# Attention steps of batches 4 to 7 moved half an output stage earlier and reordered, with four more seven-product pairs, in a fused attention and bilinear-FFN kernel

## The chip, the cores and the metric

The kernel runs on one core of a Trainium2 chip. A core has TensorE (matmuls, PE in the profile, weight loads PEld), VectorE (DVE), ScalarE (ACT), GpSimd (POOL) and SyncE (SP), each with its own instruction stream, which it works through in the order in which the program lists it; semaphores make one engine wait for another. The metric is the device time of one execution in microseconds (us), the median of several runs.

## The reference

Sparse attention for 8 batches of 8 heads (576 tokens, head size 64), then a bilinear feed-forward block over all 4608 tokens:

```python
scores = scale * np.matmul(q, k.transpose(0, 1, 3, 2))
rel = pos[:, None] - pos[None, :]
mask_local = (rel >= 0) & (rel < stride)                       # heads 0 to 3
mask_strided = (rel >= 0) & (pos[None, :] % stride == pos[:, None] % stride)   # heads 4 to 7
attn = softmax of the masked scores
x = (attn @ v), heads side by side: 4608 x 512
out = ((x @ w_a) * (x @ w_b)) @ w_out          # 512 -> 1536 -> 512
```

## The kernel before

**Feed-forward.** The tokens are cut into nine tiles of 512 (t = 0 to 8). A tile has sixteen slots, numbered 16t to 16t+15 in one list that the loop at L1122 walks. Slots 0 to 11 are the *ab stage* (`ffn_ab`, L620): slot f makes the 128-wide column block f of x@w_a and x@w_b, eight matmuls of 512 columns, ScalarE copies the first bank out (L638) and VectorE multiplies it with the second into `pf` (L641). Slots 12 to 15 are the *output stage* (`ffn_ys`, L930, with `y_plan`, L871): 84 matmuls of 256 columns (L886) in fourteen blocks of six, in the order of `Y_ORDER` (L859). "y n" below is the point after block n. ScalarE copies and VectorE adds between the blocks; the sums that these products need (`fast_s`) are made by VectorE during the ab stage.

**Seven-product pairs.** For some pairs g of column blocks (2g and 2g+1) the x@w_a half is made from seven half-size products instead of eight (a Strassen-Winograd scheme over two halves of the tokens and two of the 512 inputs): 14 matmuls of 256 columns in place of 8 of 512; the x@w_b half stays as it is. `a_pair_mid` (L676) does it in tiles 3 to 6 where `MID_A` (L28) lists g, with its shared bank `X` in the PSUM pool "e" of one buffer; `a_pair` (L736) does it in tiles 7 and 8 (`FAST_A`). ScalarE makes five copies of 256 columns instead of two of 512, and VectorE three more additions (L710). Products of differences of x need `xsum` (L668), four VectorE subtractions a tile.

**Attention.** The attention of batch b = 3 to 7 is threaded into the feed-forward matmuls of tile b-1. Its steps have letters: `S`u (L425) scores of unit u, that is matmuls into the one bank "st", an exp on ScalarE and a mask on VectorE; `V`u (L490) the product with v. Units 0 to 3 are local heads: V writes PSUM bank "o" and VectorE takes a reciprocal (L470) and multiplies out of the bank into `xl` (L488). Units 4 to 7 are strided heads (`step_VT`, L510): V writes banks "o" and "e", ScalarE does Ln, Ln, Exp (L533, L534), VectorE two products into `xT` (L536). From tile 3 on "o" and "e" have one buffer each. `Q`0 and `Q`1 copy the transposed q of the local heads into the two halves of the zero-padded buffer `qz` that S0 to S3 read, `Q`2 and `Q`3 those of the strided heads, for S4 to S7 (`step_Q`, L334, VectorE, L338). `O`c and `I`c (L500, L506) send the local result through DRAM and back, transposed, into `xT`, on SP's queue. `step_D` (L321), on the same queue, brings kT and qT by transposing DMAs. The loads of k, q and v are issued by GpSimd, which first copies one element of the slot's result (`pace`, L1134) to wait for it.

**What sets the order.** `tc.manual_schedule` keeps the order in which the code emits instructions, on every engine. In one slot come the matmuls and their copies, with the "y n" steps inside an output stage as they are reached (L893); then `soon` (fast_s), then the steps of `LATER` at that slot (`take`, L1137), then the entries of `at` (L1138: fast_s, xsum, stores, step_D). A key x of `LATER` stands for slot 16(b-1)+x, so -4 is slot 12 of tile b-2; `IN_Y` gives points inside the output stage of tile b-1.

Of the kernel before, what the change touches and what calls it, by code (L numbers as in the profile page):

```python
# [14 lines left out]
FIRST_D = 2  # L15
# [9 lines left out]
VW = 128  # L25
WCH = (0, 2, 5, 9, 12)
FAST_Y = (1, 2, 3, 4, 5, 6, 7, 8)
MID_A = {t: (1, 3) for t in (3, 4, 5, 6)}  # L28
FAST_A = {7: (1, 2, 3, 4, 5), 8: (0, 1, 2, 3, 4, 5)}


@with_exitstack
def kernel(
# [20 lines left out]
    NT = n_tok // TTOK  # L54
# [279 lines left out]
    def step_Q(b, z, j):  # L334

        r = slice(64 * j, 64 * j + 64)
        dst = qz_buf[b % 2][j][z][r]
        nc.vector.tensor_copy(dst.rearrange("d c r n -> d (c r n)") if z else dst, qT[z][r])  # L338
# [220 lines left out]
    def step_X(b, c):  # L559
# [15 lines left out]
    STEPS = {1: {5.5: "Tk2", 6: "Tq2", 7: "S4 Tk3", 7.5: "S5", 8: "Tq3", 8.5: "V4", 9: "S6 V5 Pk0", 9.5: "S7 Pq0",  # L575
# [4 lines left out]
    LATER = {-4: "Q0", -3: "Q1", -1: "S0", 0: "S1", 1: "V0", 2: "S2 Q2", 3: "V1 O0", 4: "S3 I0 Q3", 5: "V2", 6: "S4", 7: "V3 O1", 8: "S5", 9: "V4 I1",  # L580
             10: "S6",
             11: "V5"}
    IN_Y = {2: "S7", 6: "V6", 11: "V7"}
    FN = {"Tk": step_Tk, "Tq": step_Tq, "S": step_S, "V": step_V, "X": step_X, "W": lambda b, n: fast_w(n, slice(0, 3)),
          "s": S_px, "m": S_m, "L": lead_vl, "O": rows_out, "I": rows_in, "Pk": lambda b, c: pair_up("k", c), "Pq": lambda b, c: pair_up("q", c),
          "Q": lambda b, n: step_Q(b, n // 2, n % 2)}

    def run(b, slot):
        for s in slot:
# [3 lines left out]
    steps = {}  # L593
# [9 lines left out]
    def mm_bank(shape):  # L603
        nm = "tp" if used[0] % 4 == 3 and used[0] >= 0 else "mm"
        used[0] += 1
        return psum4[nm].tile(shape, F32, tag=nm, name="mm")
# [13 lines left out]
    def ffn_ab(t, f, mid, ab=None):  # L620
        if f == 0:
            pfs[t] = fsb.tile([128, FD, TTOK], BF16, tag="pf", name="pf", bufs=1)
        pf = pfs[t]
        if f // 2 in FAST_A.get(t, ()) + MID_A.get(t, ()):
            if f % 2 == 0:
                pairs[t, f // 2] = (a_pair_mid if t in MID_A else a_pair)(t, f // 2)
            return next(pairs[t, f // 2])
# [14 lines left out]
        else:  # L642
# [5 lines left out]
    xsum = {t: qz_flat[1][t - 7][:, :8 * HT].rearrange("p (n c m) -> p n c m", n=4, c=2)  # L648
            for t in FAST_A}
    xsum_mid = const.tile([128, 4, 2, HT], BF16, name="xsum")  # L650
    for t in MID_A:
        xsum[t] = xsum_mid
# [15 lines left out]
    def xsum_make(t, n):  # L668
        s_ = xsum[t]
        a, b = ((x_part(t, 0, 1), x_part(t, 0, 0)), (x_part(t, 1, 1), s_[:, 0]), (x_part(t, 1, 1), x_part(t, 0, 1)),  # L670
                (x_part(t, 1, 0), s_[:, 1]))[n]
        nc.vector.tensor_tensor(s_[:, n], a, b, op=ALU.subtract)
# [3 lines left out]
    def a_pair_mid(t, g):  # L676

        pf = pfs[t]
        X = psum4["e"].tile([128, 512], F32, tag="e", name="e")[:, :HT]
        Y, Z, b1, b0 = [mm_bank([128, TTOK]) for _ in range(4)]  # L680
        Y, Z = Y[:, :HT], Z[:, :HT]
        a = [fsb.tile([128, TTOK], F32, tag="a_sb", name="a_sb", bufs=3) for _ in range(2)][::-1]
        p7 = fsb.tile([128, HT], F32, tag="p7", name="p7")
        quarter = lambda e, k: a[e][:, HT * k:HT * (k + 1)]

        def P(bank, lhs, rhs, start=False):
            for c in range(2):
                nc.tensor.matmul(bank, lhsT=lhs(c), rhs=rhs(c), start=start and c == 0, stop=c == 1, skip_group_check=True)

        w = lambda e, j: (lambda c: wav[:, j, c, g, e])  # L690
        ws = lambda n: (lambda c: wsum_a[n][:, c, g])
        x = lambda j, k: (lambda c: x_part(t, j, k)[:, c])
        xs = lambda n: (lambda c: xsum[t][:, n, c])

        def b_mm(bank, e, kks):
            f = 2 * g + e
            x0 = TTOK * t % (XR * S)
            for kk in kks:
                for k in range(2) if x0 + TTOK > XR * S else (None,):
                    rhs = x_part(t, kk // 2, k)[:, kk % 2] if k is not None else xT[:, kk, x0:x0 + TTOK]  # L700
                    dst = bank if k is None else bank[:, HT * k:HT * (k + 1)]
                    nc.tensor.matmul(dst, lhsT=wb_sb[:, kk, 128 * f:128 * (f + 1)], rhs=rhs,  # L702
                                     start=kk == 0 and k in (None, 0), stop=kk == KD - 1 and k in (None, 1))

        def mult(e, bank):
            halves = lambda v_: v_.rearrange("p (a i s) -> p a i s", i=2, s=16)
            nc.vector.tensor_mul(pf[:, 2 * g + e, :].rearrange("p (i a s) -> p a i s", i=2, s=16), halves(a[e]), halves(bank))

        def add(q, other):
            nc.vector.tensor_tensor(q, other, q, op=ALU.add)  # L710

        P(Y, w(0, 1), x(1, 0), True)
        P(X, w(0, 0), x(0, 0), True)
        nc.scalar.copy(quarter(0, 0), X)
        b_mm(b1, 1, (0, 1, 2))
        P(X, ws(1), xs(1))
        nc.scalar.copy(quarter(1, 0), X)
        P(Z, ws(2), xs(2), True)
        nc.scalar.copy(p7, Z)
        b_mm(b1, 1, (3,))  # L720
        add(quarter(0, 0), Y)
        yield p7[:1, :1]
        P(X, ws(0), xs(0))
        nc.scalar.copy(quarter(1, 1), X)
        b_mm(b0, 0, (0,))
        P(Z, w(1, 1), xs(3))
        add(quarter(1, 0), Z)
        add(quarter(1, 1), p7)
        b_mm(b0, 0, (1, 2, 3))
        P(X, ws(3), x(1, 1))  # L730
        nc.scalar.copy(quarter(0, 1), X)
        mult(1, b1)
        mult(0, b0)
        yield pf[:1, 2 * g, :1]
# [136 lines left out]
    def y_plan(t):  # L871

        plan, y = products(t), y_bufs()
        late = t in FAST_A
        if late:
# [101 lines left out]
    with tc.manual_schedule(engines={ENG.PE, ENG.SP, ENG.Pool, ENG.DVE, ENG.Activation}):  # L977
# [30 lines left out]
        for nm in ORDER:  # L1008
            if nm[0] == "*":
                spin(int(nm[1:]))  # L1010
            elif nm == "C0":
                for x, cp, n in ((raw[0], nc.vector.tensor_copy, "k"), (raw[1], nc.scalar.copy, "q")):
                    t = nats[0, n, False][:, 0:2].rearrange("p h r d -> p (h r d)")
# [40 lines left out]
        for t in range(NT):  # L1054
            slots += [(ffn_ab, t, f) for f in range(FD)] + [(ffn_ys if t in FAST_Y else ffn_y, t, j) for j in range(4)]
        for b in range(1, B):
            for pos, names in (STEPS.get(b) or {16 * (b - 1) + x: n for x, n in LATER.items()}).items():
                steps.setdefault(pos, []).append((b, names.split()))
            if b not in STEPS:
                for n, names in IN_Y.items():  # L1060
                    steps["y", b - 1, n] = [(b, names.split())]

        at = {}

        def do(i, fn, *args):
            at.setdefault(i, []).append(lambda: fn(*args))

        soon = {}
        for t in FAST_Y[:-1]:
            if t not in FAST_A:  # L1070
                soon[16 * t + 10] = [lambda t=t: fast_s(t, 2, slice(4, 6))]
# [5 lines left out]
        for b in range(FIRST_D, B):  # L1077
            g0 = 16 * (b - 2)
            if b == FIRST_D:
                do(0, load_qk, b, False)  # L1080
                do(1, load_qk, b, True)
                do(14, load_vl, b)
                for h in range(HL):
                    do((16, 18, 19, 20)[h], load_vs, b, (h,))
            else:
                do(19 if b == FIRST_D + 1 else g0 - 2, load_qk, b, False)
                do(21 if b == FIRST_D + 1 else g0 + 2, load_qk, b, True)
                for h in range(HL):
                    do(g0 + h + (15 if b == FIRST_D + 1 else 10), load_vs, b, (h,))
                do(g0 + (12 if b == FIRST_D + 1 else 7), load_vl, b)  # L1090
            gs = {2: (13, 14, 15, 15), 3: (6, 6, 14, 15)}.get(b) or (3, 4, 10, 11)
            for (z, nm), g in zip(((0, "k"), (0, "q"), (1, "k"), (1, "q")), gs):
                do(g0 + g, step_D, b, z, nm)
        for n in range(4):
            for c in range(2):
                do(16 * 2 + (2, 5, 7, 9, 11, 13, 14, 15)[2 * n + c], wsum_make, n, c)
        for t in MID_A:
            do(16 * t - 1, xsum_make, t, 0)
            for n in (1, 2, 3):
                do(16 * t, xsum_make, t, n)  # L1100
        do(16 * (NT - 2) - 1, xsum_make, NT - 2, 0)
        for n in (2, 1, 3):
            do(16 * (NT - 2), xsum_make, NT - 2, n)
        for n in range(4):
            do(16 * (NT - 2) + 12 + n, xsum_make, NT - 1, n)
        for h in range(HL):
# [15 lines left out]
        for i, (fn, t, j) in enumerate(slots):  # L1122
            if i == 0:
                used[0] = -1000 * 3
            elif i == 16:
                used[0] = 0
            elif i == 16 * min(MID_A):
                outs.close()
# [39 lines left out]
```

## Time and profile before

| what | us |
|---|---|
| median of three runs (all: 330.45, 323.25, 323.65) | 323.65 |
| the profiled execution, whole | 323.88 |
| its span, first to last instruction | 322.2 |
| TensorE busy in the span | 313.8 |
| ab stage of tiles 3, 4, 5, 6 (starts 126.83, 160.24, 193.72, 226.99) | 23.2, 23.3, 23.1, 23.1 |
| output stage of tiles 2, 3, 4, 5, 6 | 10.2, 10.2, 10.2, 10.2, 9.9 |

The stages are read from TensorE's timeline, by the first matmul of each. A matmul's duration holds its own pipeline latency (379 ns for 512 columns, 273 ns for 256), while the next one starts after 0.216 us or 0.109 us, so TensorE's need is read from the starts. VectorE is busy 248.4 us and ScalarE 191.4 us of the span.

### The profile page before, as it was taken

How to read it: one execution, taken by the hardware profiler on the slowest of the kernel's cores; microseconds unless marked ns; L12 is line 12 of the kernel's file. 1: busy time of each engine (PE TensorE's matmuls, PEld its weight loads, DVE VectorE, ACT ScalarE, POOL GpSimd, SP SyncE). 2: the span in 40 equal slices, each digit the busy share in tenths (PEclk: the TensorE clock that was granted, in tenths of full speed). 3: DMA queues.
4: the chain of work that ended last, by engine and by line, in shares of the span. 5: the costliest groups of instructions: out<-in, count | busy, mean ns of one | idle time of the engine just before them, and what ended most of it. 6: DMA issues, size and time to landing. Idle time of an engine off the chain costs nothing. (4 is left out here: it accounts for less than half of the span.)

```text
span 322.2 us, 7287 instructions
## 1 busy us (share of the span) xinstructions
PE 313.8 (97%) x2738; PEld 217.9 (68%) x2766; DVE 248.4 (77%) x569; ACT 191.4 (59%) x371; POOL 120.2 (37%) x211
## 2 busy tenths in 40 slices
PE   8999999999999999999999999999999999999994
PEld 7764555455775578556999996559655866786684
DVE  6665797488867988899689868997799667857862
ACT  6763767355854476557655766577656655535541
POOL 8844850881255344315340435134001003203520
PEclk9999999999999999999999999999999999999999
DMA  8999999999599999999997999999235040004004
GB/s 154 146 203 199 203 190 209 174 146 152 119 126 144 209 148 104 144 157 172 123 120 151 164 108 131 158 203 135 18 85 121 2 127 5 0 4 130 3 0 130
DMA packets 127811, 40.41 MB, mean 125 GB/s; under 512 B 115616, under 2 KB 124896, under 8 KB 127584
## 3 DMA queue, kind: packets, MB, share of 16 engines
q0 software_dynamic: 80400, 19.28, 65.3%
q1 hardware_dynamic: 47232, 20.61, 35.9%
q8 instruction: 21, 0.34, 0.5%
q14 instruction: 14, 0.11, 0.1%
q10 hardware_dynamic: 144, 0.07, 0.1%
HBM read 39.12 MB, written 18.28 MB: 178 GB/s over the span
## 5 line engine op out<-in xcount | busy, mean ns | idle before, releaser
L617 PE MATMUL mm<-xT,wb_sb 128*128 128x512 bf16 (+1 forms) x301 | 71.6, 357 | 0.4
L617 PE MATMUL mm<-xT,wa_sb 128*128 128x512 bf16 (+1 forms) x287 | 70.2, 356 | 0.6
L638 ACT COPY a_sb<-mm 128x512 f32<-128x512 f32 x68 | 39.7, 584 | 29.5 <-PE mm L617 27.8
L1134 POOL CAST pace<-pf 1x1 f32<-1x1 bf16 x68 | 18.5, 273 | 87.6 <-DVE pf L641 41.0
L617 PEld LDWEIGHTS <-wb_sb 128*128 128x128 bf16 x312 | 30.0, 98 | 27.8 <-issue 0.7
L641 DVE TENSOR_TENSOR pf<-a_sb,mm 128x512 bf16<-128x512 f32 x58 | 39.4, 680 | 9.4 <-ACT a_sb L638 5.7
L401 ACT ACTIVATE p<-st 72x576 bf16<-72x576 f32 (+1 forms) x56 | 36.4, 650 | 15.4 <-PE st L381 14.7
L617 PEld LDWEIGHTS <-wa_sb 128*128 128x128 bf16 x312 | 27.9, 98 | 17.8
L886 PEld LDWEIGHTS <-ps 128*128 128x128 bf16 x336 | 32.6, 98 | 4.1 <-issue 0.5
L886 PE MATMUL mm<-wf,ps 128*128 128x256 bf16 x252 | 30.0, 273 | 0.3 <-ACT y_sb L851 0.3
L851 ACT COPY y_sb<-mm 128x512 f32<-128x512 f32 (+1 forms) x32 | 17.9, 558 | 19.1 <-PE mm L886 16.4
L1134 POOL COPY pace<-y_sb 1x1 f32<-1x1 f32 x21 | 8.4, 401 | 51.2 <-DVE y_sb L849 23.6
L886 PEld LDWEIGHTS <-pf 128*128 128x128 bf16 x252 | 23.6, 98 | 2.7
L766 PE MATMUL mm<-xT,wb_sb 128*128 128x512 bf16 x83 | 25.3, 379 | 0.1
L241 POOL DMA_DIRECT2D vs<-in_v_dram x24 | 21.7, 905 | 4.1 <-issue 1.7
L886 PE MATMUL mm<-wo_sb,pf 128*128 128x256 bf16 x168 | 21.8, 273 | 0.0
L820 DVE TENSOR_TENSOR ps<-pf 128x512 bf16<-128x512 bf16 (+1 forms) x49 | 19.6, 399 | 0.8
L702 PE MATMUL mm<-xT,wb_sb 128*128 128x512 bf16 (+1 forms) x80 | 19.1, 337 | 0.0
L419 DVE TENSOR_TENSOR p<-p,mask_l 128x576 int16<-128x576 int16 x32 | 14.5, 452 | 5.6 <-ACT p L401 5.5
L536 DVE TENSOR_TENSOR xT<-o,xr 64x288 bf16<-64x288 f32 x16 | 7.6, 477 | 13.5 <-ACT xr L534 13.4
L462 PEld LDWEIGHTS <-p 128*128 128x128 bf16 (+1 forms) x256 | 12.9, 97 | 7.1 <-DVE xl L488 1.1
L488 DVE TENSOR_TENSOR xl<-o,rc 96x384 bf16<-96x384 f32 x24 | 13.3, 553 | 0.8
(212 smaller groups left out, 644.0 us busy)
## 6 DMA issues: line engine op xcount, KB each, us to landing
out_dram<-y_sb SPq DMA_DIRECT2D x14, 512.0 KB, 4.6
kr<-in_k_dram POOLq DMA_DIRECT2D x12, 288.0 KB, 6.2
qr<-in_q_dram POOLq DMA_DIRECT2D x12, 288.0 KB, 7.1
vl<-in_v_dram POOLq DMA_DIRECT2D x6, 384.0 KB, 9.3
out_dram<-y_sb SPq DMA_DIRECT2D x7, 256.0 KB, 5.5
vs<-in_v_dram POOLq DMA_DIRECT2D x24, 72.0 KB, 4.9
xd<-xl SPq DMA_DIRECT2D x12, 144.0 KB, 3.3
wo_sb<-in_moe_w_out_dram POOLq DMA_DIRECT2D x4, 384.0 KB, 10.7
```

The lines of the kernel that those rows point to most:

```text
L241: nc.gpsimd.dma_start(out=vs_buf[b % 2][:, h, :, 0:D], in_=v[b, HL + h].rearrange("(p r) d -> p r d", r=RS))
L401: nc.scalar.activation(p_flat(p)[:M, :2 * W].rearrange("p (i n) -> p i n", n=2 * n), st[:M].rearrange("p a (i n) -> p (a i) n", n=256)[:, ...
L419: nc.vector.tensor_tensor(pi, pi, mk, op=ALU.bitwise_and)
L617: nc.tensor.matmul(ps_[:, c0:c0 + n], lhsT=w[:, kk, 128 * f:128 * (f + 1)], rhs=xT[:, kk, x0:x0 + n], start=(kk == first and c0 == 0), sto ...
L638: nc.scalar.copy(a_sb, ab[0])
L641: nc.vector.tensor_mul(pf[:, f, :].rearrange("p (i a s) -> p a i s", i=2, s=16), halves(a_sb), halves(ab[1]))
L702: nc.tensor.matmul(dst, lhsT=wb_sb[:, kk, 128 * f:128 * (f + 1)], rhs=rhs, start=kk == 0 and k in (None, 0), stop=kk == KD - 1 and k in (N ...
L766: nc.tensor.matmul(got[e], lhsT=wb_sb[:, kk, 128 * f:128 * (f + 1)], rhs=xT[:, kk, x0:x0 + TTOK], start=kk == 0, stop=kk == KD - 1)
L820: nc.vector.tensor_tensor(s[:, n], a, b, op=op)
L851: nc.scalar.copy({"1": part(0, 0), "7": part(0, 1), "6": part(1, 0), "5": part(1, 1)}[k], bank)
L886: nc.tensor.matmul(bank[b][:, q], lhsT=lhs(g, q), rhs=rhs(g), start=k in "172" and q == 0 and g == 0, stop=g == FG - 1, skip_group_check=True)
L1134: nc.gpsimd.tensor_copy(pace, done)
```

## The change

The dictionary `LATER` held for batches 3 to 7; now batch 3 keeps it under the name `THIRD`, and batches 4 to 7 get a new one. In it Q0 and Q1 stand after slots 11 and 12 of tile b-2, S0 at y 4 and S1 at y 7 of that tile's output stage, Q2 and Q3 after slot 13, S4 at y 12, V0 at y 13; V6 moves into the ab stage (slot 10), V7 to y 2; V4, V5, V6 stand at slots 2, 6, 10 and are mixed with V1, V2, V3. The four sums `xsum` are taken from the tile's first slots to y 7 and y 9 of the stage before. The strided transposes of step_D are emitted at slot 8 instead of 10 and 11. `MID_A` goes from pairs 1 and 3 in each of tiles 3 to 6 to pairs 2 and 4 in tile 3 and 0, 2 and 4 in tiles 4 to 6; tile 7 gets pair 0 as well: four seven-product pairs more in all. In `a_pair_mid` two banks change places for g = 0, and one matmul of the x@w_b half is put before the fifth product.

```diff
-MID_A = {t: (1, 3) for t in (3, 4, 5, 6)}
-FAST_A = {7: (1, 2, 3, 4, 5), 8: (0, 1, 2, 3, 4, 5)}
+MID_A = {3: (2, 4), 4: (0, 2, 4), 5: (0, 2, 4), 6: (0, 2, 4)}
+FAST_A = {7: (0, 1, 2, 3, 4, 5), 8: (0, 1, 2, 3, 4, 5)}
...
-    LATER = {-4: "Q0", -3: "Q1", -1: "S0", 0: "S1", 1: "V0", 2: "S2 Q2", 3: "V1 O0", 4: "S3 I0 Q3", 5: "V2", 6: "S4", 7: "V3 O1", 8: "S5", 9: "V4 I1",
-             10: "S6",
-             11: "V5"}
-    IN_Y = {2: "S7", 6: "V6", 11: "V7"}
+    THIRD = {-4: "Q0", -3: "Q1", -1: "S0", 0: "S1", 1: "V0", 2: "S2 Q2", 3: "V1 O0", 4: "S3 I0 Q3", 5: "V2", 6: "S4", 7: "V3 O1", 8: "S5",
+             9: "V4 I1", 10: "S6", 11: "V5", ("y", 2): "S7", ("y", 6): "V6", ("y", 11): "V7"}
+    LATER = {-5: "Q0", -4: "Q1", ("y", -10): "S0", ("y", -7): "S1", -3: "Q2 Q3", ("y", -2): "S4", ("y", -1): "V0",
+             0: "S2", 1: "V1 O0", 2: "V4 S3", 3: "V2 S5 I0", 5: "V3 O1", 6: "V5 S6", 7: "I1", 9: "S7", 10: "V6",
+             ("y", 2): "V7", ("y", 7): "x0 x1", ("y", 9): "x2 x3"}
...
         Y, Z, b1, b0 = [mm_bank([128, TTOK]) for _ in range(4)]
+        if g == 0:
+            Z, b1 = b1, Z
...
+        b_mm(b0, 0, (0,))
         P(X, ws(0), xs(0))
         nc.scalar.copy(quarter(1, 1), X)
-        b_mm(b0, 0, (0,))
+        b_mm(b0, 0, (1,))
         P(Z, w(1, 1), xs(3))
         add(quarter(1, 0), Z)
         add(quarter(1, 1), p7)
-        b_mm(b0, 0, (1, 2, 3))
+        b_mm(b0, 0, (2, 3))
...
+                if isinstance(pos, tuple):
+                    pos = ("y", b - 1, pos[1]) if pos[1] > 0 else ("y", b - 2, 14 + pos[1])
...
-            gs = {2: (13, 14, 15, 15), 3: (6, 6, 14, 15)}.get(b) or (3, 4, 10, 11)
+            gs = {2: (13, 14, 15, 15), 3: (6, 6, 14, 15)}.get(b) or (3, 4, 8, 8)
...
-        for t in MID_A:
-            do(16 * t - 1, xsum_make, t, 0)
-            for n in (1, 2, 3):
-                do(16 * t, xsum_make, t, n)
-        do(16 * (NT - 2) - 1, xsum_make, NT - 2, 0)
-        for n in (2, 1, 3):
-            do(16 * (NT - 2), xsum_make, NT - 2, n)
+        do(47, xsum_make, 3, 0)
+        for n in (1, 2, 3):
+            do(48, xsum_make, 3, n)
```

More of the change, by code (lines that the diff above doesn't have):

```diff
@@ L579 @@
                  24: "V3 I0 O1", 24.5: "S5", 25.5: "V4", 26: "S6", 26.5: "I1", 27: "V5", 27.5: "S7", 28.5: "V6", 30: "V7"}}
-    LATER = {-4: "Q0", -3: "Q1", -1: "S0", 0: "S1", 1: "V0", 2: "S2 Q2", 3: "V1 O0", 4: "S3 I0 Q3", 5: "V2", 6: "S4", 7: "V3 O1", 8: "S5", 9: "V4 I1",
-             10: "S6",
-             11: "V5"}
-    IN_Y = {2: "S7", 6: "V6", 11: "V7"}
+    THIRD = {-4: "Q0", -3: "Q1", -1: "S0", 0: "S1", 1: "V0", 2: "S2 Q2", 3: "V1 O0", 4: "S3 I0 Q3", 5: "V2", 6: "S4", 7: "V3 O1", 8: "S5",
[3 more added lines that the diff above has]
+             ("y", 2): "V7", ("y", 7): "x0 x1", ("y", 9): "x2 x3"}
     FN = {"Tk": step_Tk, "Tq": step_Tq, "S": step_S, "V": step_V, "X": step_X, "W": lambda b, n: fast_w(n, slice(0, 3)),
           "s": S_px, "m": S_m, "L": lead_vl, "O": rows_out, "I": rows_in, "Pk": lambda b, c: pair_up("k", c), "Pq": lambda b, c: pair_up("q", c),
-          "Q": lambda b, n: step_Q(b, n // 2, n % 2)}
+          "Q": lambda b, n: step_Q(b, n // 2, n % 2), "x": lambda b, n: xsum_make(b, n)}
     def run(b, slot):
@@ L1056 @@
         for b in range(1, B):
-            for pos, names in (STEPS.get(b) or {16 * (b - 1) + x: n for x, n in LATER.items()}).items():
+            for pos, names in (STEPS.get(b) or (THIRD if b == FIRST_D + 1 else LATER)).items():
+                if isinstance(pos, tuple):
+                    pos = ("y", b - 1, pos[1]) if pos[1] > 0 else ("y", b - 2, 14 + pos[1])
+                elif b not in STEPS:
+                    pos += 16 * (b - 1)
                 steps.setdefault(pos, []).append((b, names.split()))
-            if b not in STEPS:
-                for n, names in IN_Y.items():
-                    steps["y", b - 1, n] = [(b, names.split())]
         at = {}
```

## The prediction, made before the changed kernel ran

> **What bounds the kernel now.** I read the page first, then the list of waits, the table of stretches, and the timelines of tiles 2 to 5. The page: TensorE is busy nearly all the span, at full clock throughout.
>
> ```profile
> PE 313.8 (97%) x2738; PEld 217.9 (68%) x2766; DVE 248.4 (77%) x569; ACT 191.4 (59%) x371; POOL 120.2 (37%) x211
> ...
> PEclk9999999999999999999999999999999999999999
> ```
>
> The list of waits (engine, line, whom it waited for, total us, times, longest) is full of the other engines waiting for TensorE; among its sixty longest rows this is the only one in which TensorE waits:
>
> ```profile
> PEld L462 <- DVE xl L488: 1.1, 2, 0.8
> ```
>
> In TensorE's timeline of tiles 3 to 7 each matmul starts 0.216 us (512 columns) or 0.109 us (256) after the one before. There is no gap to win back there. So fewer columns are a gain one for one, and any new wait on TensorE is a loss one for one. The table of stretches (us, then busy time of PE, PEld, DVE, ACT, POOL) for tile 4, ab and output stage, says where room is:
>
> ```profile
> 160.20:183.50 23.30, 23.30 (x252) 21.19 (x250) 20.56 (x49) 14.33 (x29) 7.64 (x16) 1.00 1.29 133
> 183.50:193.70 10.20, 10.20 (x113) 9.26 (x110) 7.40 (x17) 7.18 (x15) 4.52 (x8) 1.00 1.34 141
> ```
>
> VectorE has 2.7 us free in the ab stage and 2.8 in the output stage: enough work time, so what counts is the length of chains, and the order in which VectorE stands in them.
>
> **The pairs.** In tile 4 the pair g = 1 runs from 164.16 to 167.69 with 0.25 us of a score step inside: 3.28 us. The two plain slots behind it take 167.87 to 169.62 and 169.87 to 171.62: 3.50 us. Four pairs more: 4 x 0.22 = **-0.9 us**. Their three additions (0.41 us each, VectorE) and 0.7 us of copies (5 x 0.37 for 2 x 0.58, ScalarE) lie beside matmuls.
>
> **S0 behind Q1 (the largest term).** S0 reads both halves of qz, so it waits for Q1. In the instruction order of the built kernel, VectorE's stream at the output stage of tiles 3, 4 and 5 reads: Q0, the two products of V7 into xT, Q1. Q1 is emitted after slot 12, and V7 at y 2 inside that slot. So S0 at y 4 waits for the whole chain of V7 at y 2, and the output matmuls stand behind S0 in TensorE's stream. The trace has this chain once a tile: V6 at y 6, then Q1. TensorE, ScalarE and VectorE in tile 4 (start, duration):
>
> ```profile
> 187.70 0.30 PE L521 MATMUL o<-p,vs 72*128 72x72 bf16 x4
> 187.96 1.48 PE L886 MATMUL mm<-wf,pf 128*128 128x256 bf16 x12
> ...
> 187.95 0.59 ACT L851 COPY y_sb<-mm 128x512 f32<-128x512 f32 x1 [0.77 <-PE mm L886]
> 188.56 0.43 ACT L533 ACTIVATE xr<-o 64x288 f32<-64x288 f32 x1
> ...
> 190.04 0.48 DVE L536 TENSOR_TENSOR xT<-o,xr 64x288 bf16<-64x288 f32 x1 [2.23 <-ACT xr L534]
> 190.42 0.46 DVE L536 TENSOR_TENSOR xT<-e,xr 64x288 bf16<-64x288 f32 x1
> 190.91 0.46 DVE L338 COPY qz0l<-qTl 64x1152 bf16<-64x1152 bf16 x1
> ```
>
> From V6's first matmul (187.70) to Q1's end (191.37) it is 3.67 us; V7 at y 2 stands behind a ScalarE copy in the same way. TensorE gets from V7 to S0 in 0.26 + 12 x 0.109 = 1.57 us. It waits 2.1 us, in three tiles. In tile 2 (S0 of batch 4) the step at y 2 is S7 of batch 3, and its mask stands before Q1; VectorE's timeline there:
>
> ```profile
> 119.11 0.75 DVE L530 TENSOR_TENSOR xT<-o,xr 64x576 bf16<-64x576 f32 x1
> 119.89 0.56 DVE L662 TENSOR_TENSOR tk<-wa_sb 128x768 bf16<-128x768 bf16 x1
> 120.37 0.45 DVE L419 TENSOR_TENSOR p<-p,mask_s 72x576 int16<-72x576 int16 x1
> 120.74 0.44 DVE L338 COPY qz0l<-qTl 64x1152 bf16<-64x1152 bf16 x1
> ```
>
> With Q0 (0.37 from start to start) now behind the first row and Q1 behind the mask, Q1 ends at 121.5; S0 is due at 116.62 + 0.25 + 24 x 0.109 = 119.5. Again 2.1. Sum **+8.4 us**; bounds 7 (VectorE 0.35 ahead each time) and 10 (S1's own chain pushed too).
>
> **V4 and V5 behind "o".** V4 (slot 2) now follows V1 (slot 1), and V5 (slot 6) follows V3 (slot 5): one plain slot between them (1.75 us), two or more before. Each needs the bank that V1 or V3 wrote, which is free once `xl` is made. Behind a seven-product pair that comes late, since the pair's two products stand first. V1 in tile 4:
>
> ```profile
> 167.69 0.34 PE L462 MATMUL o<-vl,p 128*128 128x65 bf16 x6
> ...
> 168.56 1.28 DVE L707 TENSOR_TENSOR pf<-a_sb,mm 128x512 bf16<-128x512 f32 x2
> 169.76 0.18 DVE L470 RECIPROCAL rc<-o 96x6 f32<-96x6 f32 x1
> 169.98 0.55 DVE L488 TENSOR_TENSOR xl<-o,rc 96x384 bf16<-96x384 f32 x1
> ```
>
> From 167.69 to 170.54: 2.85 us. A copy Q (0.37) no longer stands among these, so 2.5. V4 is due 0.18 + 1.75 = 1.93 after V1: a wait of 0.55 in tiles 4 to 6 (tile 3 has plain slots there, where the same chain took 1.95): **+1.7 us**. V3's pair has no score mask in it, so VectorE may be ahead there; bounds 0 and 0.9, and I take 0.35 in tiles 3 to 6: **+1.4 us**.
>
> **Bank "e", and the rest.** The pair of slots 8 and 9 writes "e" 0.26 + 0.25 + 1.75 + 0.22 = 2.48 us after V5's start; V4 in tile 4 had released it after 2.66 (179.25 to 181.91). With 0.06 for the signal: 4 x 0.25 = **+1.0 us** (0 to 2). At the head of tiles 4 to 7 the pair's second use of X waits for a ScalarE copy that follows the last output copy: 0.15 each, **+0.6** (0 to 1.5). The bank swap for g = 0 makes that pair's third product reuse the last bank freed; the product comes 1.3 us after the stage's end, and the copy (0.58) covers it, so nothing. The moved matmul changes only the order. Moving the sums takes four subtractions (0.42 each) from the crowded ab stage into the output stage's free 2.8 us: nothing, if I1 has landed.
>
> **DMAs.** SP's queue gets I0 right behind O0 (which it must wait out: 2 to 4 us idle, once covered by a transpose and a store), then transpose, store, transpose, store, O1, I1, and the five strided transposes; the loads on GpSimd's queue keep their places. Q2 and Q3 now come 3 slots earlier against the end of that queue. In tile 4 O1 was issued at 180.51, I1 at 187.80, the last transpose about 195.2, and Q2 ran at 200.84. With V1 two slots earlier O1 goes out some 17 to 19 us after the tile's start instead of 20, and with I1 4 to 7 us behind it the last of these lands 32 to 39 us after; Q2 is due on VectorE at about 33. **+0.5 us**, bounds 0 and 6 for each of tiles 3 to 5.
>
> **Sum:** -0.9 + 8.4 + 1.7 + 1.4 + 1.0 + 0.6 + 0.5 = +12.7 us. The profiled execution took 323.88 (span 322.2 and 1.7 around it), 0.23 over the median: 336.6 for it, 336.3 for the median, so **336 us**.
>
> **Rivals.**
> *The waits are covered, not slower.* It needs Q1 to end before S0 is due, that is a V7 chain of 1.57 us instead of 3.67; for it speaks that VectorE idles 2.2 us before V6's products, against it that this idle time is the chain itself (Ln, Ln, Exp on ScalarE). Only the saving would be left: 322.8. It decides from a wait per tile under about 1.6 us with all smaller ones gone, which would be within 2%. Chance 0.12.
> *The transposes end last.* If O1 falls behind the load of v, as in tile 4 (7.3 us to I1), S4 at y 12 waits 4 to 6 us more in tiles 3 to 5: 336 + 15 = 351, with two such tiles 346. For it: the same 7 us show in tile 3 (145.84 to 152.90); against it: 4.9 us in tile 5, and O1 is now issued before that load (18 us into the tile). Chance 0.12.
> *The clock falls.* A wait long enough could halve the granted clock; in the trace the first 224-column matmuls start 0.19 us apart and later ones 0.10, and the one gap of 0.6 us (before 42.05) left the clock at 1.00. If each of the four waits of 2.1 us brought a stretch of 3 us at half speed, 4 x 1.5 = 6 us more: 342. Chance 0.06. [...]
>
> **How the numbers follow.** The forecast has 0.70: S0's waits alone give 331, all bounds high 343. The covered case is left out below, and part of the transposes' case above: 328 to 346. What a measurement of this kernel can tell from no change is 2%, that is 317.2 and 330.1. Faster: 0.02, from the covered case with more gained than I see. Within 2%: 0.10 of the covered case and 0.05 of the forecast, 0.15. Slower: 0.83.
>
> **What would show it.** TensorE gaps of about 2 us before L381 at y 4 in tiles 2 to 5, ended by VectorE's L338; gaps of 0.3 to 0.6 us before L521 at slots 2 and 6, ended by L488; a wait row for both that is absent today; PEclk at 9 all along. It is wrong if S0 starts on time, if the gaps before S4 (y 12, ended by a transpose) are the larger, or if TensorE's own matmul time fell by more than 0.9 us.

## The result and the profile after

The changed kernel takes 345.71 us in the median of four runs (342.0 to 348.46), beside 324.41 for the kernel before, run on the same chip. The ratio is 1.058 (95% interval 1.048 to 1.067); like all ratios here it leaves out executions that count as disturbed, here the two of 348.0 and 348.5 us. Its profiled execution took 343.43 us with a span of 341.6, that is 19.4 us more than the 322.2 of before. The page, the rows for TensorE and for the granted clock:

```profile
PE 318.8 (93%) x2751; PEld 219.3 (64%) x2782; DVE 253.8 (74%) x580; ACT 193.3 (57%) x383; POOL 121.0 (35%) x204
...
PEclk9999999999999989999999999999999999999999
```

TensorE fell from 97% to 93% of the span: the time was added as idle time, apart from one slice (the 8) with a lower clock. Among its sixty longest rows the list of waits now has four in which TensorE waits for VectorE, where the kernel before had one, of 1.1 us:

```profile
PE st L381 <- DVE qz0l L338: 4.4, 2, 2.2
PE st L381 <- DVE qz1l L338: 4.4, 2, 2.2
PE o L521 <- DVE xl L488: 3.3, 7, 0.6
PEld L691 <- DVE xT L536: 1.4, 4, 0.4
```

The reader is to see S0 (L381 with a local qz) waiting four times for Q1, V4 and V5 (L521) seven times for the bank that `xl` frees, and the pairs (L691; the new lines push L688 to L691) four times for bank "e". The table of stretches for tile 4, ab stage and output stage, has the same columns as before:

```profile
169.20:193.80 24.60, 23.73 (x248) 20.45 (x247) 19.80 (x47) 15.81 (x36) 8.75 (x16) 1.00 1.14 146
193.80:206.50 12.70, 10.51 (x110) 9.39 (x109) 9.72 (x22) 6.14 (x11) 3.63 (x7) 1.00 1.08 92
```

The output stage grew by 2.5 us (10.2 to 12.7) and the ab stage by 1.3 (23.3 to 24.6), although three pairs replace two. Tiles 3 and 5 show the same (output 10.2 to 12.7 and 13.7, ab 23.2 and 23.1 to 24.2 and 24.5); tile 2's output stage went from 10.2 to 15.8. A part of each difference is only that steps changed their stage: S0, S1, S4 and V0 now stand in the output stage. Here is S0 in tile 4's output stage, from the timelines of TensorE, ScalarE and VectorE:

```profile
195.16 0.29 PE L521 MATMUL o<-p,vs 72*128 72x72 bf16 x4
...
195.41 1.48 PE L890 MATMUL mm<-wf,ps 128*128 128x256 bf16 x12
199.08 0.41 PE L381 MATMUL st<-qz0l,kT0l 128*128 128x192 bf16 x3 [2.19 <-DVE qz0l L338]
...
195.40 0.59 ACT L855 COPY y_sb<-mm 128x512 f32<-128x512 f32 x1 [1.17 <-issue]
196.01 0.44 ACT L533 ACTIVATE xr<-o 64x288 f32<-64x288 f32 x1
...
196.23 0.44 DVE L338 COPY qz0l<-qTl 64x1152 bf16<-64x1152 bf16 x1
197.50 0.47 DVE L536 TENSOR_TENSOR xT<-o,xr 64x288 bf16<-64x288 f32 x1 [0.82 <-ACT xr L534]
197.88 0.46 DVE L536 TENSOR_TENSOR xT<-e,xr 64x288 bf16<-64x288 f32 x1
198.35 0.68 DVE L338 COPY qz0l<-qTl 64x1152 bf16<-64x1152 bf16 x1
```

This is the predicted chain: V7 at y 2, ScalarE's Ln behind an output copy, Q0 done at 196.67 (S0 is due at 196.73), VectorE idle 0.82 us for the Exp, V7's two products, then Q1, then S0. From V7's first matmul to Q1's end it is 3.87 us (predicted 3.67), and Q1 took 0.68 us where 0.46 was read from the kernel before.

In the following table a gap is what a TensorE start comes later than the columns of the matmuls before it explain; gaps under 0.15 us are left out.

| term | predicted us | measured us |
|---|---|---|
| pairs | -0.9 | -0.9 (3.28 each: in tile 5 206.56 to 210.09 without 0.25 for a score step) |
| S0 behind Q1, tiles 2 to 5 | 8.4 | 9.5 (2.42, 2.38, 2.36, 2.38) |
| V4 behind "o" | 1.7 | 2.2 (0.2, 0.49, 0.74, 0.73) |
| V5 behind "o" | 1.4 | 2.5 (0.62, 0.60, 0.63, 0.62) |
| bank "e" | 1.0 | 1.0 (0.25, 0.23, 0.25, 0.25) |
| heads of tiles, other banks, V2 | 0.6 | 0.8 |
| S4 behind the transposes | 0.5 | 1.0 (once, tile 5) |
| V0 of batch 4 in tile 2 | none | 0.8 (131.45) |
| half clock, 122.87 to 126.28 | none in the sum | 1.7 |
| sum | 12.7 | 18.6 of 19.4 |

### The profile page after: what moved, and what is told of

Read it like the earlier page. It is cut to its first block, busy times and chain, and to the rows that moved or that the text cites. A ratio compares the mean times of both kernels' runs of the same rounds, so it can differ in the third digit from the quotient of the medians.

```text
span 341.6 us, 7329 instructions
## 1 busy us (share of the span) xinstructions
PE 318.8 (93%) x2751; PEld 219.3 (64%) x2782; DVE 253.8 (74%) x580; ACT 193.3 (57%) x383; POOL 121.0 (35%) x204
## 4 chain that ended last, share of the span: by engine, by line
PE 70%; DVE 12%; ACT 7%; DMA 3%; issue 3%; POOL 2%; SPq 1%; DVEq 0%; POOLq 0%; ACTq 0%
PE mm L618 22%; PE mm L890 14%; PE mm L770 5%; PE mm L705 4%; PE st L381 3%; PE ax L763 3%; PE mm L952 3%; DVE pf L710 3%; PE e L691 2%; PE mm L763 2%; PE o L462 2%; DMA vl<-in_v_dram 2%; DVE xT L536 2%; PE mm L691 2%; PE mm L917 2%
## 5 line engine op out<-in xcount | busy, mean ns | idle before, releaser
L618 PE MATMUL mm<-xT,wb_sb 128*128 128x512 bf16 (+1 forms) x258 | 61.7, 359 | 0.4
L618 PE MATMUL mm<-xT,wa_sb 128*128 128x512 bf16 (+1 forms) x250 | 60.8, 358 | 0.6
L639 ACT COPY a_sb<-mm 128x512 f32<-128x512 f32 x60 | 35.0, 583 | 24.8 <-PE mm L618 23.0
L618 PEld LDWEIGHTS <-wb_sb 128*128 128x128 bf16 x272 | 26.1, 98 | 24.9 <-issue 0.4
L642 DVE TENSOR_TENSOR pf<-a_sb,mm 128x512 bf16<-128x512 f32 x50 | 34.0, 680 | 8.1 <-ACT a_sb L639 4.3
L618 PEld LDWEIGHTS <-wa_sb 128*128 128x128 bf16 x272 | 24.1, 98 | 16.0
L890 PE MATMUL mm<-wf,ps 128*128 128x256 bf16 x252 | 31.1, 275 | 0.3 <-ACT y_sb L855 0.3
L770 PE MATMUL mm<-xT,wb_sb 128*128 128x512 bf16 x90 | 27.4, 379 | 0.1
L890 PEld LDWEIGHTS <-pf 128*128 128x128 bf16 x252 | 24.6, 100 | 4.1 <-DVE pf L775 0.3
L705 PE MATMUL mm<-xT,wb_sb 128*128 128x512 bf16 (+1 forms) x110 | 26.3, 332 | 0.0
L1135 POOL COPY pace<-y_sb 1x1 f32<-1x1 f32 x17 | 5.3, 314 | 52.1 <-DVE y_sb L853 33.9
L241 POOL DMA_DIRECT2D vs<-in_v_dram x24 | 21.8, 910 | 3.5 <-issue 2.0
L419 DVE TENSOR_TENSOR p<-p,mask_l 128x576 int16<-128x576 int16 x32 | 14.4, 451 | 10.0 <-ACT p L401 9.6
L521 PEld LDWEIGHTS <-vs 72*128 72x128 bf16 x192 | 9.1, 99 | 8.6 <-issue 6.6
```

What stands on the lines that cost most here:

```text
L241: nc.gpsimd.dma_start(out=vs_buf[b % 2][:, h, :, 0:D], in_=v[b, HL + h].rearrange("(p r) d -> p r d", r=RS))
L618: nc.tensor.matmul(ps_[:, c0:c0 + n], lhsT=w[:, kk, 128 * f:128 * (f + 1)], rhs=xT[:, kk, x0:x0 + n], start=(kk == first and c0 == 0), sto ...
L639: nc.scalar.copy(a_sb, ab[0])
L642: nc.vector.tensor_mul(pf[:, f, :].rearrange("p (i a s) -> p a i s", i=2, s=16), halves(a_sb), halves(ab[1]))
L770: nc.tensor.matmul(got[e], lhsT=wb_sb[:, kk, 128 * f:128 * (f + 1)], rhs=xT[:, kk, x0:x0 + TTOK], start=kk == 0, stop=kk == KD - 1)
L890: nc.tensor.matmul(bank[b][:, q], lhsT=lhs(g, q), rhs=rhs(g), start=k in "172" and q == 0 and g == 0, stop=g == FG - 1, skip_group_check=True)
```

## The experiments

All runs are compared with the kernel before on the same chip, whose medians there were 323.5 to 323.8 us.

**Q1 ahead of V7.**

```diff
-    LATER = {-5: "Q0", -4: "Q1", ("y", -10): "S0",
+    LATER = {-5: "Q0 Q1", ("y", -10): "S0",
```

> Edit: Q1 stands right behind Q0 (after slot 11), ahead of V7's products in VectorE's stream; nothing else. Theory A (S0's four waits of 2.4 us are Q1's place in VectorE's order): in the changed kernel's trace Q0 begins at 233.47 in tile 5, so Q1 would end at 234.3 where S0 is due at 233.9: the wait falls to about 0.5 us in tiles 3 to 5 and 1.2 in tile 2, 6.9 us less, and no stretch at half clock (1.7 us less); some 2 to 4 us of it come back before S4, since Q2 reaches the strided transposes 2 us earlier (they landed at 165.96, 203.30 and 241.85): 336 to 340. Rival B (the DMA transposes end last): everything gained at S0 is waited out at S4: 341 to 343. Rival C (the loss is half-clock stretches, not the wait): S0's gap goes but the time falls only by the 1.7 us of the clock: 341.7.

Measured: 347.18 us, ratio 1.069 (1.059 to 1.078), no better than the change. The waits of TensorE:

```profile
PE st L381 <- DVE qz0s L338: 4.5, 2, 2.8
...
PE st L381 <- DVE qz0l L338: 1.9, 2, 1.5
PE st L381 <- DVE qz1s L338: 1.9, 2, 1.1
PE o L462 <- DVE xT L530: 1.9, 1, 1.9
PE st L381 <- DVE qz1l L338: 1.0, 2, 0.5
```

S0's gaps (rows with qz0l and qz1l) fell from 9.5 to 3.6 us in all. But S4 (rows qz0s and qz1s) now waits in every tile, 1.83, 0.91, 2.98 and 1.31 us (7.0 instead of 1.0), because its q arrives by the transposes on SP's queue, which did not come sooner here: in tile 4 Q2 starts at 206.62 us, beside 203.42 in the changed kernel. VectorE's row for Q2 and Q3 there:

```profile
206.62 0.92 DVE L338 COPY qz0s<-qTs 64x1152 bf16<-64x1152 bf16 x2 [3.84 <-DMA qTs<-qr]
```

What was gained at S0 (5.9 us) was waited out at S4 (6.0 us more), which is what rival B said; the time lies above all three expectations, for V0 in tile 2 waits 2.0 us instead of 0.8, and the profile holds two stretches at half clock instead of one (PEclk 8 in two slices, mean clock 0.990). So a second chain lay beside S0's, almost as long: removing the first one alone gains nothing.

**V1 and V3 a slot earlier.**

```diff
-             0: "S2", 1: "V1 O0", 2: "V4 S3", 3: "V2 S5 I0", 5: "V3 O1",
+             0: "S2 V1", 1: "O0", 2: "V4 S3", 3: "V2 S5 I0", 4: "V3", 5: "O1",
```

> Edit: V1 stands after slot 0 instead of 1 and V3 after slot 4 instead of 5, in the middle of their seven-product pairs; O0 and O1 stay. Theory A (V4 and V5 wait for bank o, whose release stands behind the pair's two products): the gaps before V4 (0.50, 0.74, 0.73 in tiles 4 to 6, 0.2 in tile 3) and V5 (0.62, 0.60, 0.63, 0.62) go: 4.3 us less, 339. Rival: the reciprocal and product of V1 and V3, now ahead of the pair's additions, make these late, and the pair's banks with them: no gain, 341 to 344.

Measured: 340.28 us, ratio 1.050 (1.040 to 1.060). TensorE's waits in the list:

```profile
PE st L381 <- DVE qz0l L338: 4.5, 2, 2.3
PE st L381 <- DVE qz1l L338: 4.4, 2, 2.2
PE o L462 <- DVE xT L530: 1.5, 1, 1.5
PEld L691 <- DVE xT L536: 1.5, 4, 0.4
```

The row L521 <- L488 is gone, the two of S0 and the one of bank "e" are as they were: V4 and V5 did wait for the bank that V1 and V3 leave. S4 waits nowhere here. What the rival named, additions of a pair that come late, shows in one place, a wait of 0.9 us in tile 4 (L618 behind L710).

**Without pair 0.**

```diff
-MID_A = {3: (2, 4), 4: (0, 2, 4), 5: (0, 2, 4), 6: (0, 2, 4)}
-FAST_A = {7: (0, 1, 2, 3, 4, 5), 8: (0, 1, 2, 3, 4, 5)}
+MID_A = {t: (2, 4) for t in (3, 4, 5, 6)}
+FAST_A = {7: (1, 2, 3, 4, 5), 8: (0, 1, 2, 3, 4, 5)}
```

> Edit: the four added seven-product pairs are taken out (pairs 2 and 4 alone in tiles 3 to 6, pairs 1 to 5 in tile 7), the new order of attention stays. Theory A: TensorE has 0.9 us more matmul work, V4's gap falls to the 0.2 us of tile 3 in tiles 4 to 6 (1.4 us less), the small gaps at the heads of tiles 4 and 7 go (0.4 less): 342 to 343, no real change; S0's and V5's gaps stay. Rival (the pairs' additions on VectorE are what makes all chains late): the gaps at S0 and V5 shrink too, 337 or less.

Measured: 346.21 us, ratio 1.068 (1.058 to 1.079): with the new order and as many pairs as before, the whole loss is there. S0's and V5's gaps stayed at 2.4 and 0.6 us, so the pairs' additions are not what makes these chains late. V4's gaps in tiles 4 to 6 shrank to 0.1 us at most, but S4 waited 1.3 to 1.5 us in three tiles, and the mean clock of the profile was 0.985 over 345.8 us, which is 5 us lost to the lower clock:

```profile
PE st L381 <- DVE qz0s L338: 2.5, 2, 1.3
PE o L462 <- DVE xT L530: 1.9, 1, 1.9
PE o L521 <- DVE xl L488: 1.8, 4, 0.5
```

**S0's wait filled.** Twenty matmuls of constants into an unused part of the score bank are put before S0 of batches 4 to 7; they change no result and take the time in which TensorE would wait.

```diff
+            if b > 3 and u == 0:
+                for _ in range(20):
+                    nc.tensor.matmul(sv[:, 3, :224], lhsT=nc.const_aps.tensor(1.0, [128, 128], BF16),
+                                     rhs=nc.const_aps.tensor(1.0, [128, 224], BF16), start=True, stop=True)
```

> Edit: 20 matmuls of constants, 224 columns each, are put before S0 in batches 4 to 7, into a part of the bank that S0 does not use; they add 2 us of TensorE work in the gap in which it waited, and are no part of the result. Theory A (the clock fell because TensorE stood idle 2.2 to 2.4 us): granted clock 1.000 in every run, the spread of 342.0 to 348.5 narrows, all runs 341 to 343. Rival (the falls are chance, or come from load): clocks of 0.985 to 0.995 in some runs and times up to 348 as before. If the wait for Q1 were not what holds S0, the 20 matmuls would add 2 us a tile: 350.

Measured: 344.83 us, ratio 1.063 (1.055 to 1.072). TensorE's timeline in tile 4:

```profile
201.37 2.14 PE L371 MATMUL st<-const-bfloat16-1.0 128*128 128x224 bf16 x20
203.74 0.41 PE L385 MATMUL st<-qz0l,kT0l 128*128 128x192 bf16 x3 [0.23 <-DVE qz0l L338]
```

Nearly 8 us of added matmuls left the time where it was, so S0's wait is time that TensorE has to spare. In tile 4 it is covered but for an idle 0.23 us, and none of the four filled places is followed by a stretch at half clock; the only slice with a lower clock before the last one, 129.3 to 138.0 us, comes with waits of 1.8 and 2.0 us in tile 2 that were not filled. So the expectation holds for the filled places, and not for the whole: the mean clocks were 0.989 to 0.999, and the times 343.6 to 346.7.

**S4 later.**

```diff
-    LATER = {-5: "Q0", -4: "Q1", ..., -3: "Q2 Q3", ("y", -2): "S4", ("y", -1): "V0",
-             0: "S2", 1: "V1 O0",
+    LATER = {-5: "Q0", -4: "Q1", ..., ("y", -1): "V0",
+             0: "S2 Q2 Q3", 1: "V1 O0 S4",
```

> Q2, Q3 and S4 of batches 4 to 7 are put one to three slots later (Q2, Q3 behind slot 0, S4 behind slot 1 of the tile, instead of slot 13 and y 12 of the stage before); Q1, S0 and all else stay as in the changed kernel. Theory (the wait of S0 on Q1, 4 x 2.4 us, holds up TensorE; S4's wait on the transposes is a second, parallel chain which ends about at the same time): S0's four waits stay at 2.2 to 2.4 us, the waits of TensorE on qz0s or qz1s (0.8 us in the changed kernel's rows) go, the wait of V0 in tile 2 may move: 341 to 343. Rival (the transposes are what matters and S0's wait is only where it shows): below 338.

Measured: 348.73 us, ratio 1.077 (1.071 to 1.084), slower than expected by either. S0's four waits stayed at 2.4 us, as the theory had it, but the new place of S4 costs more than it saves:

```profile
PE st L381 <- DVE qz0l L338: 4.5, 2, 2.3
PE st L381 <- DVE qz1l L338: 4.4, 2, 2.2
PE o L521 <- DVE p L419: 3.0, 4, 0.9
PE o L521 <- DVE xl L488: 1.8, 4, 0.5
```

V4 (L521 <- L419) now waits 0.7 to 1.1 us for the mask of S4's probabilities, one slot behind it; S4 itself waits 0.5 to 0.6 us, since Q2 and Q3 stand behind the mask of S2 on VectorE, which in tile 4 waits 1.38 us for ScalarE's exp:

```profile
174.99 0.46 DVE L419 TENSOR_TENSOR p<-p,mask_l 128x576 int16<-128x576 int16 x1 [1.38 <-ACT p L401]
175.36 0.92 DVE L338 COPY qz1s<-qTs 64x1152 bf16<-64x1152 bf16 x2
```

And three of the four S0 waits were followed by half clock (PEclk 8 in three slices, mean clock 0.985).

**S4 later and Q1 first.** The last two edits together, `-5: "Q0 Q1"` and Q2, Q3, S4 behind slots 0 and 1.

> The last edit (Q2, Q3 behind slot 0, S4 behind slot 1) together with Q1 right behind Q0, both behind slot 11. Either edit alone takes one chain away and leaves the other. Theory (two chains side by side): S0's waits fall from 9.5 to about 3.6 us in all, as with Q1 first alone, and the 7.0 us of waits before S4 that came with it go too; with the half-speed stretches gone as well: 333 to 337. Rival (moving work among VectorE's steps only pushes the waits further, for instance Q2 waiting for its transpose then holds up the pair's additions): 340 or more.

Measured: 338.48 us (338.04 to 339.69), ratio 1.047 (1.044 to 1.050), a little above the theory's range and below the rival's. TensorE's waits:

```profile
PE o L521 <- DVE p L419: 3.0, 4, 0.9
PE st L381 <- DVE qz0l L338: 1.9, 2, 1.5
PE o L521 <- DVE xl L488: 1.8, 4, 0.5
```

This settles the two chains. Putting Q1 first gained nothing in the changed kernel (ratio 1.058 without it, 1.069 with it), and 10.2 us where S4 does not depend on a late transpose (348.7 to 338.5); some 5 us of that are three stretches at half clock in the profile of the one and none in that of the other. The rest of the miss is V4 behind S4's mask and S4 behind S2's, 3.7 and 2.3 us, which the theory had left out.

**Only V7 moved.** S4 later, Q1 where the change puts it, and V7 from y 2 to y 5, behind S0 on TensorE.

```diff
-             ("y", 2): "V7",
+             ("y", 5): "V7",
```

> S4, Q2 and Q3 later as in that kernel alone (which left S0's waits at 2.4 us four times), Q1 where the change puts it, and only V7 moved, from y 2 to y 5 of the output stage, behind S0 in TensorE's order. Theory (S0 waits because Q1 stands behind V7's two products on VectorE): the three waits of S0 in tiles 3 to 5 fall from 2.4 to at most 0.7 us, as with Q1 moved ahead, while the one in tile 2, where the step at y 2 is a score step of batch 3, stays at 2.4; 338 to 341. Rival (Q1 is late for another reason, such as its own transpose): all four stay, 347 to 349.

Measured: 341.47 us (340.01 to 344.19), ratio 1.056 (1.049 to 1.063).

```profile
PE st L381 <- DVE qz0l L338: 3.0, 2, 2.3
PE o L521 <- DVE xl L488: 1.8, 4, 0.5
PE st L381 <- DVE qz1l L338: 1.5, 2, 0.8
```

S0's gaps are 2.42 in tile 2, where y 2 holds a score step of batch 3 and nothing was moved, and 0.92, 0.90, 0.92 in tiles 3 to 5, a little over the 0.7 of the theory and far from the rival's 2.4. So it is V7's chain on VectorE that held Q1 up there, and not the arrival of q: moving V7 away works without touching Q1. The time is half a microsecond above what was expected.

**All of it.** The kernel with Q1 first and S4 later gets V1 and V3 a slot earlier; then S0 and S1 at y 6 and y 10 as well, V0 of batch 4 behind slot 0, and the second and third product of the pairs of tiles 3 to 6 exchanged:

```diff
-             0: "S2 Q2 Q3", 1: "V1 O0 S4", ..., 5: "V3 O1",
+             0: "S2 V1 Q2 Q3", 1: "O0 S4", ..., 4: "V3", 5: "O1",
...
-    ("y", -10): "S0", ("y", -7): "S1",
+    ("y", -8): "S0", ("y", -4): "S1",
...
+        b_mm(b1, 1, (0,))
         P(X, w(0, 0), x(0, 0), True)
         nc.scalar.copy(quarter(0, 0), X)
-        b_mm(b1, 1, (0, 1, 2))
-        P(X, ws(1), xs(1))
-        nc.scalar.copy(quarter(1, 0), X)
+        b_mm(b1, 1, (1, 2))
         P(Z, ws(2), xs(2), True)
         nc.scalar.copy(p7, Z)
+        P(X, ws(1), xs(1))
+        nc.scalar.copy(quarter(1, 0), X)
```

With V1 and V3 alone:

> The last kernel with V1 and V3 one slot earlier as well (V1 behind slot 0, V3 behind slot 4), which by itself took the 0.5 and 0.6 us waits for bank o away. Theory (these waits are independent of the two chains): 4 us less than the last kernel, 329 to 332. Rival (what is won there is given back at S0 or S4): no less than the last kernel by more than 1 us.

Measured: 336.36 us, ratio 1.041 (1.038 to 1.044). The rows of the list:

```profile
PE st L381 <- DVE qz1s L338: 2.3, 2, 1.1
PE st L381 <- DVE qz0s L338: 2.1, 2, 1.1
PE st L381 <- DVE qz0l L338: 1.9, 2, 1.5
```

V5's waits for `xl` are gone, and V4's for the mask fell from 3.7 to under 1 us in all, but S4's rose from 0.5 to 0.6 us per tile to 1.2 to 1.3: V1's `xl` now stands ahead of Q2 and Q3 on VectorE. Half of the 4 us came back, so the theory that these waits are independent fell, and so did the rival's 1 us. With all the edits:

> The last kernel with S0 two blocks later (y 6) and S1 three blocks later (y 10), V0 of batch 4 behind slot 0 instead of y 13, and in the seven-product pairs of tiles 3 to 6 one x@w_b matmul put ahead of the first product and the second and third product exchanged. Theory: every wait of TensorE over 0.3 us is then gone and what is left is the saving of four pairs, 0.9 us, less bank e: 323 to 327, and no stretch at half clock. Rival (S0 and S1 so late bring the probabilities late, so that V0 or the exp and mask of the next units end last): 328 or more, with waits before L462 or L521 on masks.

Measured: 335.04 us, ratio 1.036 (1.031 to 1.042), a miss of 8 us. The four waits of S0 are gone, while those of S4 (0.7 and three times 1.3 us) and V4 (0.7, 0.4, 0.4) stay, and two banks in tiles 3 and 4 cost 0.5 each. Tile 3's first slot waits 0.8 us for `xT` by DMA. So the rival had the time right, but only 1.5 us of it are waits on masks. This profile also holds 2.5 us of waits for `tq` (L285) before 45 us, far from every edit; the kernel before has 0.8 of them. No version of the new order tried here came within 3% of the kernel before.

**More pairs in the old order.** The kernel before, with one more pair (2) in each of tiles 3 to 6:

```diff
-MID_A = {t: (1, 3) for t in (3, 4, 5, 6)}
+MID_A = {t: (1, 2, 3) for t in (3, 4, 5, 6)}
```

> The kernel before with its own order of the attention steps, and one more seven-product pair, of slots 4 and 5, in each of tiles 3 to 6 (pairs 1, 2, 3): as many pairs more as the change has, in places where no strided product uses bank e. Theory (the pairs are worth 0.22 us each, the order is what costs): 322.6 to 323.0 beside 323.7 for the kernel before. Rival (a third pair in a row puts VectorE behind, so that the local products' xl comes late for the next product in bank o): 324.5 or more, with TensorE waits on L488.

Measured: 329.9 us (328.85 to 331.9), ratio 1.018 (1.014 to 1.023). TensorE's timeline in tile 4, at the seam of two pairs, then the row of the list:

```profile
174.88 0.38 PE L688 MATMUL e<-xT,wa_sb 128*128 128x256 bf16 x2
176.42 0.83 PE L702 MATMUL mm<-xT,wb_sb 128*128 128x256 bf16 x6 [1.17 <-DVE pf L707]
```

```profile
PE mm L702 <- DVE pf L707: 3.6, 4, 1.2
```

The time is 1.8% longer, as the rival said, but not by its mechanism: there is no new wait on L488. A pair takes four matmul banks and bank "e", and the next pair begins with the same ones while VectorE is still multiplying the last two out (L707, 1.28 us for both). The saving of 0.22 us per pair stands against a wait of 0.8 and 1.3 us at the two seams of tiles 3 and 4, and of several gaps of 0.2 to 0.3 in tiles 5 and 6. With a plain slot between pairs, as in the change, this wait is not there.

## Why the prediction was right in kind and short in size

The forecast of 336 us named the direction, the places and the order of the terms; the median is 9.7 us higher, near the top end of the range, and the executions of 342.0 and 343.4 us lie 6 to 7 above the forecast. No term came out smaller than taken, so no luck of cancelling terms is in it.

- **What bounds it.** TensorE had no gap to win back, and each new wait was a loss one for one: right, the table accounts for 18.6 of the 19.4 us.
- **The pairs.** Right, 3.28 us each in the changed kernel too.
- **S0 behind Q1.** Right in mechanism: the run with only V7 moved shows that it is V7's chain in tiles 3 to 5. The term was mis-sized by 1.1 us, since a wait was 2.4 and not 2.1. Most of that is Q1's copy, 0.68 to 0.70 us in tiles 3 to 5 and 0.56 in tile 2 in place of 0.44 to 0.46; the rest is 0.05 to 0.15 us from its end to S0's start. What the long copies have in common is in the last section.
- **V4 and V5 behind "o".** Right: their row disappears when V1 and V3 come a slot earlier. V5 was taken at 0.35 and measured 0.62, inside its bounds of 0 and 0.9; the reason given for the low value, that VectorE would be ahead, does not help. In tile 4 it was ahead (it idled 0.35 us before an addition of V3's pair, at 181.12), but the chain begins with the pair's last product, and from V3 to the end of `xl` it took 2.38 us, beside 2.49 for V1. V4 came to 2.2 where 1.7 was predicted: `xl` ends 2.49 us after V1 begins in tiles 4 and 5, as taken, but V4 starts another 0.15 us later, and tile 3, taken at nothing, has 0.2.
- **Bank "e".** Right, 1.0 us in four gaps of 0.23 to 0.25.
- **DMAs.** 1.0 us instead of 0.5, in one tile of the three. TensorE and VectorE at S4 in tile 5:

```profile
243.04 0.41 PE L381 MATMUL st<-qz1s,kT1s 128*128 128x144 bf16 x4 [0.82 <-DVE qz1s L338]
...
241.97 0.92 DVE L338 COPY qz1s<-qTs 64x1152 bf16<-64x1152 bf16 x2 [1.85 <-DMA qTs<-qr]
```

  VectorE waited 1.85 us for the transpose, and TensorE only the last 0.8 of it. The price was near, but the rival it belonged to was misjudged: the transposes and the S0 chain were told as separate additions, while they run side by side. In the changed kernel S0's wait hides the transposes, and they show as soon as S0 is early.
- **Left out.** V0 of batch 4 stands at y 13 behind the last strided product of batch 3, which the old order still runs in tile 2: 0.8 us here, up to 2.0 in other runs.
- **The clock.** The sum kept it at full; it was named as a rival with 0.06. It fell once in the profiled execution, to 0.50 for 3.41 us (the rival had 3 us at half speed behind each wait), at a cost of 1.7 us, behind S0's wait in tile 2, so the sign "PEclk at 9 all along" failed in one slice. The executions of 342.0 and 343.4 us had mean clocks of 1.000 and 0.995; at full clock, then, the miss is 5 to 6 us, 4.2 of it the difference of the other terms in the table. The last section has the measured stretches.

In the working, "all bounds high 343" comes to 342 with the bounds as given (-0.9 + 10 + 1.7 + 3.6 + 2 + 1.5 + 0.5 over 323.65), and it leaves out the bound of 6 us for the transposes in each of three tiles.

What stays open: the 0.8 us that the table does not reach, which lie in gaps too small to tell from the records.

## What to carry to other kernels

When a step is moved earlier, find the last thing that stands ahead of its input in the program order of the engine that makes it, and count the whole chain of that thing (here V7's matmul, two Ln, an Exp, two products) from where it begins. When a wait is found, ask what it hides before pricing its removal: an engine that waits longest shows only the chain that ends last, and the one beside it, 1.0 us in the profile, was worth 7.0 once the first was gone. A cheaper block is worth its saving only where its banks come free in time; 0.22 us saved by a pair was lost several times over in a wait of 0.8 to 1.3 us at a seam.

## What the runs showed of the hardware

The half-clock stretches had been given a chance of 0.06. In the changed kernel the granted clock was 0.50 from 122.87 to 126.28 us, that is for 3.41 us. The table of stretches around S0 in tile 2, cut at steps of that length from its start (us, then busy time of PE, PEld, DVE, ACT, POOL, the granted clock, DMA share, GB/s):

```profile
119.46:122.87 3.41, 1.16 (x12) 1.03 (x12) 2.82 (x6) 1.21 (x2) 1.93 (x4) 1.00 1.99 152
122.87:126.28 3.41, 3.41 (x25) 2.66 (x24) 0.64 (x2) 1.94 (x4) 0.00 (x0) 0.50 1.68 122
126.28:129.70 3.42, 3.42 (x38) 3.10 (x37) 3.25 (x7) 1.69 (x3) 0.00 (x0) 1.00 0.00 0
```

The same for the wait in tile 5 of the kernel with S4 later, which is as long (2.38 us) but lies across a cut; the steps there are counted from 122.40, where a stretch at 0.50 begins in that trace:

```profile
238.43:241.84 3.41, 2.43 (x28) 2.05 (x27) 2.54 (x8) 2.40 (x5) 2.11 (x4) 1.00 1.43 189
241.84:245.26 3.42, 2.18 (x21) 1.99 (x21) 2.88 (x7) 1.24 (x3) 0.93 (x2) 1.00 2.56 82
245.26:248.60 3.34, 3.34 (x34) 3.01 (x33) 2.21 (x6) 1.44 (x3) 0.00 (x0) 1.00 0.49 28
```

The step with 1.16 us of busy TensorE is followed by one at half clock, and the two with over 2 us each are not. Stretches of 3.4 us in the traces, by TensorE's busy time and the clock granted in the stretch behind them:

| kernel | from | TensorE busy us | clock behind it |
|---|---|---|---|
| S4 later | 118.99 | 1.15 | 0.50 |
| the changed kernel | 119.46 | 1.16 | 0.50 |
| V1 and V3 a slot earlier | 157.40 | 1.19 | 0.51 |
| V1 and V3 a slot earlier | 232.54 | 1.37 | 0.50 |
| only V7 moved | 118.90 | 1.38 | 1.00 |
| V1 and V3 a slot earlier | 194.98 | 1.50 | 1.00 |
| the changed kernel | 160.41 | 2.08 | 1.00 |

At 1.37 and 1.38 us one was followed by half clock and one was not, and no run shows what decides it. In the changed kernel a wait of 2.42 us (tile 2) came with 1.7 us more for 3.41 us at 0.50, and one of 2.38 us (tile 3, the last row) with none. The executions without pair 0, which keeps four waits over 2 us, spread by more, 344.5 (mean clock 0.990) to 349.2 (0.978), than those with Q1 first and S4 later, where no such wait is left: 338.0 to 339.7 (0.999 to 1.000).

Q1's long copy has a companion. GpSimd in tile 4 of the changed kernel, while Q1 ran from 198.35 to 199.03; the second of the two issues ends at 198.77:

```profile
197.17 1.60 POOL L241 DMA_DIRECT2D vs<-in_v_dram  x2
```

Of the 48 copies of this shape (L338, 64x1152) in the traces of the kernel before and of the changed one, six took 0.56 to 0.70 us and the others at most 0.46. In each of the six an issue of a load of v on GpSimd (L241) ended while the copy ran, and in none of the 42 others. Two of the six stand in the kernel before, at 153.33 and 220.07. No run moved a load by itself, so whether the issue holds up the copy is not shown.
